# Router logits of a fused attention, mixture-of-experts and channel-mix kernel: stationary and moving operands swapped onto four column tiles, counts in three products, scatters through disjoint views

## The chip, the cores and the metric

The kernel runs on one core of one Trainium2 chip. A NeuronCore has five engines, each with its own queue of instructions: TensorE (PE; its weight loads are listed apart as PEld), VectorE (DVE), ScalarE (ACT), GpSimd (POOL) and SyncE (SP, which here only issues DMAs). The metric is the device time of one execution in microseconds, lower is better. Of several runs the median counts.

## The reference

Three stages follow one another, for a batch of 2 and a sequence of 768, all in fp32.

```python
# attention: 8 heads of 64, causal window of 96 keys plus 8 global keys, a bias by distance
scores = q @ k.T / 8 - slope[h] * dist ; masked ; a = softmax(scores) ; x = a @ v     # x: [2, 768, 512]
# mixture of experts: 8 experts, one of them for each token
logits = x @ w_gate                        # [.., 8]
local  = sigmoid(x @ w_local)              # [.., 1]
for each batch, for s in order:
    fresh = argmax(logits[s])
    e = fresh if s == 0 or local[s] < 0.5 else e_of_the_token_before
    out[s] = softmax(logits[s])[e] * (relu(x[s] @ w1[e]) @ w2[e])
# channel mix
xk, xr = mixes of x with the token before ; k = relu(xk @ w_k) ; y = sigmoid(xr @ w_r) * (k*k @ w_v)
```

A token may inherit the expert of the token before it, so routing needs a scan over the tokens in order. Since the softmax of the attention divides by a sum for each head, the kernel keeps x undivided and multiplies the logits of each head with that head's reciprocal.

## The kernel before, in words

The 1536 tokens are 12 tiles of 128. The attention part is a software pipeline over 24 iterations `i`, two for each tile (`t, g = divmod(i, 2)`, four heads each). In an iteration PE issues the transposes of the probabilities of the iteration before (`emit_pT`, lines 899 and 901, two PSUM banks of the name PT in turn), scores for later iterations (`emit_S`, line 866) or the transposes of the next k and q (line 823), and at every second iteration the products of probabilities and v (`emit_pv`, line 924), which run on two column tiles of 64. ACT does the exponentials (line 892), half of the evictions of transposed probabilities (`pt`, line 908; DVE does the other half, line 910) and the evictions of the transposed attention output `xT` (line 929). DVE adds the bias and takes the minimum (line 880). At odd iterations PE turns `xT` back (`turn_x`, line 182, into a bank PT) and DVE multiplies it into `X` (`route_x`, line 186), which empties that bank.

Routing runs beside this for groups of two tiles, six groups in all. Their steps are put at named points of later iterations (`at(i, point, ...)`; in an iteration the points come in the order Ra, Dm, Rb, Db, Rc, Dc), so the order on every engine is fixed by the program text. The steps that matter here:

- `route_lg` (line 200), at Rb of iteration `2 * g[-1] + 3`: for each of the two tiles four products with `xT` (128x128) as the stationary operand and a block-diagonal `wgb` of 18 columns (two heads, 8 experts and the local gate each) as the moving one. The result has tokens on partitions, and heads and experts along the free dimension.
- `route_max` (line 206 and after), at Dm of the next iteration: DVE scales by the reciprocals and adds over the heads.
- `route_rows`, `route_scan`, `route_turn`, `route_oh`: the scan over tokens on one partition, then a one-hot of the chosen expert (`OHr`).
- `route_sum` (lines 273 to 279): running counts of tokens for each expert, by products of one-hots with triangles of ones (`tri[:, 0]` lower triangle, `tri[:, 1]` all ones), with `acc` the sum of earlier groups. For two tiles these are five products of 8 columns (three in the first group, which has no `acc`), then the total counts.
- `route_pos`, then `scatter` (line 283): POOL writes the rows of X into `xs` in DRAM, sorted by expert. A scatter is issued where the queue `scq` holds one, at most one at each of two points of an iteration. After scatters 7 and 9 SP loads early rows of `xs` (line 948). The scatters all write the one tensor `xs`, so each waits for the one before it to land.

All the small PSUM results of routing share one bank of the name R. The sixth group is handled in the tail, where its logits are written with `route_lg` between products of the first expert. After that come the experts (products in three parts of fp32r, lines 641 to 643, with weights split by ACT at line 625 and by DVE), then the channel mix.

Of the kernel before, what the change touches and what calls it, by code (L numbers as in the profile page):

```python
# [7 lines left out]

F32 = mybir.dt.float32
# [3 lines left out]
ACTF = mybir.ActivationFunctionType  # L13
ALU = mybir.AluOpType
AX = mybir.AxisListType

P = 128
B, H, S, HD = 2, 8, 768, 64
D, E, F = 512, 8, 1024
NT = S // P  # L20
NTT = B * NT
KD = D // P
# [20 lines left out]
ROWS = sum(CAPS)  # L43
PRE = P
FREE = 4
NIN = 4
NI = 2 * NTT
NTAB = (5, 4)
# [5 lines left out]
class Net:  # L54
# [29 lines left out]
    def routing_consts(self):  # L84
        nc, c = self.nc, self.const
        self.wg = c.tile([P, KD, E + 1], F32, name="wg")
        nc.sync.dma_start(out=self.wg[:, :, 0:E], in_=self.i["w_gate"].rearrange("(k p) e -> p k e", p=P))
        nc.sync.dma_start(out=self.wg[:, :, E:E + 1], in_=self.i["w_local"].rearrange("(k p) e -> p k e", p=P))
        self.wgb = c.tile([P, KD, 2, E + 1], F32, name="wgb")
        nc.gpsimd.memset(self.wgb, 0.0)  # L90
        self.LS = c.tile([P, NTT, E + 1], F32, name="LS")
        self.RI = c.tile([P, NTT, H], F32, name="RI")
        self.MX = c.tile([P, NTT], F32, name="MX")
        self.OHr = c.tile([P, NTT, E], F32R, name="OH")
        self.OH = self.OHr.bitcast(F32)
        self.POS = c.tile([P, NTT], F32, name="POS")
        self.posi = c.tile([P, NTT], I32, name="posi")
        self.yposi = c.tile([P, NTT], I32, name="yposi")
        self.PE = c.tile([P, NTT], F32, name="PEX")
        self.caps = c.tile([8, E], F32, name="caps")  # L100
        self.bases = c.tile([8, E], F32, name="bases")
        nc.vector.memset(self.caps, 256.0)
        for r in (0, THIRD) + HALF:
            nc.vector.memset(self.caps[:, r:r + 1], float(CAPS[r]))
        nc.vector.tensor_scalar(self.bases, self.iota_e[0:8, :], 256.0, float(BASES[3] - 768), op0=ALU.mult, op1=ALU.add)
        nc.vector.memset(self.bases[:, 0:1], 0.0)
        for r in (1, 2) + tuple(range(HALF[0] + 1, E)):
            nc.vector.memset(self.bases[:, r:r + 1], float(BASES[r]))
        self.places = c.tile([8, E], F32, name="places")
        for p, k in enumerate(PLACES):  # L110
            nc.gpsimd.memset(self.places[:, p:p + 1], float(k))
        self.last = c.tile([8, E], F32, name="last")
        nc.vector.memset(self.last, float(P))
        nc.vector.memset(self.last[:, THIRD:THIRD + 1], float(LAST))
        self.second = c.tile([8, E], F32, name="second")
        nc.vector.memset(self.second, float(P))
        for r in HALF:
            nc.vector.memset(self.second[:, r:r + 1], float(LAST))
        self.elast = None
# [17 lines left out]
    def gate_rest(self):  # L137
        for a in range(2):
            r = slice(a * HD, (a + 1) * HD)
            self.nc.gpsimd.tensor_copy(self.wgb[r, :, a, :], self.wg[r, :, :])  # L140

    def mix_rest(self):
        for m in self.mu.values():
# [50 lines left out]
    def route_lg(self, g, t, xT, tag="R"):  # L194
        nc = self.nc
        if t == g[0]:
            self.lgp = self.bank(tag, 2 if tag == "PT" else 1)
        for kk in range(KD):
            o = ((t - g[0]) * H + 2 * kk) * (E + 1)
            nc.tensor.matmul(self.lgp[:, o:o + 2 * (E + 1)], lhsT=xT[:, kk, :],  # L200
                             rhs=self.wgb[:, kk, :, :].rearrange("p a c -> p (a c)"), start=True, stop=True)

    def route_max(self, pool, g):
        nc, n, t0 = self.nc, len(g), g[0]
        lh = pool.tile([P, n * H, E + 1], F32, tag="lh", bufs=1, name=f"lh{t0}")
        nc.vector.tensor_tensor(lh, self.lgp[:, 0:n * H * (E + 1)].rearrange("p (a c) -> p a c", c=E + 1),
                                self.RI[:, t0:t0 + n, :].rearrange("p a h -> p (a h)").unsqueeze(2).to_broadcast([P, n * H, E + 1]), op=ALU.mult)
        lp = self.LS[:, t0:t0 + n, :]
        nc.vector.tensor_reduce(lp, lh.rearrange("p (a h) c -> p a c h", h=H), axis=AX.X, op=ALU.add)
        mx = self.MX[:, t0:t0 + n]  # L210
        nc.vector.tensor_reduce(mx, lp[:, :, 0:E], axis=AX.X, op=ALU.max)
        ab = pool.tile([P, 2, n], F32, tag="ab", bufs=2, name=f"ab{t0}")
        fl = pool.tile([P, n], F32, tag="fl", bufs=2, name=f"fl{t0}")
        nc.vector.tensor_scalar(ab[:, 0, :].unsqueeze(2), lp[:, :, E:E + 1], ZCUT, None, op0=ALU.is_gt)
        eq = pool.tile([P, n, E], F32, tag="eq", bufs=2, name=f"eq{t0}")
        nc.vector.tensor_tensor(eq, lp[:, :, 0:E], mx.unsqueeze(2).to_broadcast([P, n, E]), op=ALU.is_ge)
        nc.vector.tensor_scalar(fl.unsqueeze(2), lp[:, :, E:E + 1], ZCUT, None, op0=ALU.is_le)
        if t0 % NT == 0:
            nc.vector.memset(ab[0:1, 0, 0:1], 0.0)
            nc.vector.memset(fl[0:1, 0:1], 1.0)  # L220
        self.mxs = (eq, ab, fl)
# [45 lines left out]
    def route_sum(self, pool, g):  # L267
        nc, n, t0 = self.nc, len(g), g[0]
        pp = self.bank("R", 1)
        for i in range(n):  # L270
            rest = [self.OHr[:, t0 + a, :] for a in range(i)] + ([self.acc] if self.acc is not None else [])
            o = pp[:, i * E:(i + 1) * E]
            nc.tensor.matmul(o, lhsT=self.tri[:, 0, :], rhs=self.OHr[:, t0 + i, :], start=True, stop=not rest)
            for a, x in enumerate(rest):
                nc.tensor.matmul(o, lhsT=self.tri[:, 1, :], rhs=x, start=False, stop=a == len(rest) - 1)
        one = self.tri[:, 1, 0:1].bitcast(F32)
        parts = [self.OHr[:, t, :].bitcast(F32) for t in g] + ([self.acc.bitcast(F32)] if self.acc is not None else [])
        for a, x in enumerate(parts):
            nc.tensor.matmul(pp[0:8, n * E:n * E + 1], lhsT=x, rhs=one, start=a == 0, stop=a == len(parts) - 1)
        self.pp = pp  # L280

    def scatter(self, X, t):
        self.nc.gpsimd.indirect_dma_start(self.xs, bass.IndirectOffsetOnAxis(ap=self.posi[:, t:t + 1], axis=0),  # L283
                                          X[t], None)

    def route_pos(self, pool, g):
# [291 lines left out]
def build(ctx, tc, ins, out):  # L578
# [2 lines left out]
    q, k, v = ins["q"], ins["k"], ins["v"]  # L581
    w1, w2 = ins["w1"], ins["w2"]
    n.xs = n.dram.tile([E * REG, D], F32, name="xs")
    ys = n.dram.tile([ROWS, D], F32, name="ys")
    rp = ctx.enter_context(tc.tile_pool(name="rp", bufs=1))
    wstack = ExitStack()
# [378 lines left out]
    def at(i, point, *fs):  # L965
        plan.setdefault((i, point), []).extend(fs)
# [2 lines left out]
        for f in plan.pop((i, point), ()):  # L969
            f()  # L970

    def lg(g):
        for t in g:
            n.route_lg(g, t, xTs[t])

    def pos(g):
        n.route_pos(ap2, g)
        scq.extend(g)
# [4 lines left out]
    for g in groups:  # L983
        i = 2 * g[-1] + 3
        lgg, mx, mx2, rows, scan, tn, oh, sm_, ps_, acc = (lambda f=f, g=g: f(ap2, g) for f in (
            lambda _, g: lg(g), n.route_max, n.route_max2, n.route_rows, n.route_scan, n.route_turn, n.route_oh, n.route_sum,
            lambda _, g: pos(g), n.route_acc))
        if g[-1] == NTT - 1:
            tail = mx, mx2, rows, scan, tn, oh, sm_, ps_
            continue  # L990
        at(i, "Rb", lgg)
        at(i + 1, "Dm", mx, mx2)
        if g[-1] == NTT - 3:
            tail8 = rows, scan, tn, oh, sm_, ps_, acc
            continue
        at(i + 1, "Rc", rows)
        if g[-1] == NTT - 5:
            at(i + 1, "Dc", scan)
            at(i + 2, "Ra", tn)
            at(i + 2, "Dm", oh)  # L1000
            at(i + 2, "Rb", sm_)
            at(i + 2, "Db", ps_, acc)
        else:
            at(i + 2, "Dm", scan)
            at(i + 2, "Rb", tn)
            at(i + 2, "Db", oh)
            at(i + 3, "Rb", sm_)
            at(i + 3, "Db", ps_, acc)
        if g[-1] in (5, 7):
            e = g[-1] == 7  # L1010
            at(i + 3, "Db", lambda e=e: n.order_a(ap2, "fg"[e], n.cnte if e else n.cnt6, n.fvec if e else None))
            at(*((i + 4, "Ra") if e else (i + 3, "Dc")), lambda e=e: n.order_b(ap2, "fg"[e], rp))
            at(i + 4, "Rb", lambda e=e: early_start(3 * e, e))

    with tc.manual_schedule():
# [96 lines left out]
        for i in range(NI - 1):  # L1112
# [46 lines left out]
                emit_pv(u, 1)  # L1159
            do(i, "Rc")  # L1160
            do(i, "Dc")
            if scq:
                scatter(scq.pop(0))
            if g == 1 and t + 2 < NTT:
                load("v", t + 2)
# [797 lines left out]
```

## Time and profile before

| what | value |
|---|---|
| median of 3 runs | 487.65 us (485.9, 487.65, 492.04) |
| the profiled execution's own time | 488.38 us |
| its span, first to last instruction | 486.3 us |
| mean granted TensorE clock | 0.99 |
| PE busy, share of the span | 469.6 us, 97% |
| PEld busy | 407.0 us, 84% |
| DVE busy | 344.4 us, 71% |
| ACT busy | 265.5 us, 55% |
| POOL busy | 114.4 us, 24% |

Matmuls are pipelined, and their ends are modelled, so what one costs in a row of them is read from the distance of the starts, not from its duration. In a timeline, `x4` means that a row holds four instructions that follow each other. `128*64 128x128` on PE means 128 rows and 64 columns of the array, with a moving operand of 128 partitions and 128 columns. A plain fp32 product shows as two instructions. The attention part ends near 118 us, the last group's routing near 134 us.

### The profile page before, as it was taken

Reading aid. Unit: us, or ns where it says so; the run is one execution under the profiler, and the core shown is the slowest. Engines: PE = TensorE matmul, PEld = TensorE weight load, DVE = VectorE, ACT = ScalarE, POOL = GpSimd, SP = SyncE. Lnnn points to the kernel's source line nnn. Section 1 sums busy time; section 2 is a strip of 40 time slices with the busy share of each in tenths; the row PEclk is TensorE's granted clock in tenths of the full one; section 3 lists DMA queues with packets and bytes.
Section 4 is the critical chain, followed back from the end, with each engine's and each line's share of the span. In section 5 each row is a group of like instructions: output and inputs, shape, how many; then the busy total and the mean of one; then the engine's idle time right before and its main releaser. Section 6 shows DMA issues by size and latency. Waiting matters only on the chain. (4 is left out here: it accounts for less than half of the span.)

```text
span 486.3 us, 9258 instructions
## 1 busy us (share of the span) xinstructions
PE 469.6 (97%) x3211; PEld 407.0 (84%) x3211; DVE 344.4 (71%) x911; ACT 265.5 (55%) x652; POOL 114.4 (24%) x200
## 2 busy tenths in 40 slices
PE   7999999889999999999999999999999999999994
PEld 5788888778788989878978887798989899898984
DVE  7877796696875885897898888797857768264301
ACT  4787876764536554757587776862433414152320
POOL 4111212112110000010010013051754918253220
PEclk9999998989999999999999999999999999999998
DMA  9998585962775978598699753003836442200001
GB/s 181 266 234 165 145 175 153 290 201 83 255 278 167 355 207 325 171 345 288 238 344 378 278 177 97 34 1 90 301 109 246 146 155 82 65 23 23 22 3 49
DMA packets 76492, 86.90 MB, mean 179 GB/s; under 512 B 50677, under 2 KB 50933, under 8 KB 76437
## 3 DMA queue, kind: packets, MB, share of 16 engines
q1 hardware_dynamic: 68176, 63.01, 42.3%
q0 software_dynamic: 4944, 17.17, 10.9%
q10 hardware_dynamic: 3316, 6.03, 3.4%
q8 instruction: 28, 0.46, 0.4%
q14 instruction: 28, 0.22, 0.2%
HBM read 73.49 MB, written 12.71 MB: 177 GB/s over the span
## 5 line engine op out<-in xcount | busy, mean ns | idle before, releaser
L625 ACT ACTIVATE whi<-wraw 128x512 fp32r<-128x512 f32 x128 | 72.5, 623 | 6.1 <-ACTq L717 2.3
L634 DVE TENSOR_TENSOR wlo<-wraw,whi 128x1024 fp32r<-128x1024 f32 x55 | 66.0, 1217 | 2.7 <-ACT whi L625 2.5
L1474 ACT ACTIVATE sq<-S 128x256 f32<-128x256 f32 x48 | 18.5, 385 | 74.4 <-PE S L643 71.3
L641 PE MATMUL S<-xkh,whi 128*128 128x256 f32 x192 | 54.5, 284 | 0.2 <-ACT whi L625 0.2
L643 PE MATMUL S<-xkh,wlo 128*128 128x256 f32 x192 | 53.6, 279 | 0.2 <-DVE wlo L630 0.2
L642 PE MATMUL S<-xkl,whi 128*128 128x256 f32 x192 | 53.5, 279 | 0.0
L1484 POOL TENSOR_TENSOR kl<-sq,kh 128x256 fp32r<-128x256 f32 x40 | 36.5, 921 | 71.1 <-issue 37.4
L1514 DVE TENSOR_TENSOR o<-O,sig 128x512 f32<-128x512 f32 (+1 forms) x13 | 8.4, 649 | 51.9 <-PE O L643 31.7
L642 PE MATMUL O<-wlo,kh 128*128 128x512 f32 (+1 forms) x104 | 39.3, 378 | 0.3 <-DVE wlo L630 0.3
L643 PE MATMUL O<-whi,kl 128*128 128x512 f32 (+1 forms) x104 | 39.3, 378 | 0.0
L641 PE MATMUL O<-whi,kh 128*128 128x512 f32 (+1 forms) x104 | 39.1, 376 | 0.0
L641 PEld LDWEIGHTS S<-xkh,whi 128*128 128x128 f32 x192 | 36.4, 190 | 0.7 <-ACT whi L625 0.4
L643 PEld LDWEIGHTS S<-xkh,wlo 128*128 128x128 f32 x192 | 36.0, 188 | 0.4 <-DVE wlo L630 0.4
L642 PEld LDWEIGHTS S<-xkl,whi 128*128 128x128 f32 x192 | 36.1, 188 | 0.3
L1475 DVE SCALAR_TENSOR_TENSOR sq<-S,sq 128x256 f32<-128x256 f32 x48 | 20.1, 420 | 16.4 <-ACT sq L1474 16.0
L1483 ACT ACTIVATE kh<-sq 128x256 fp32r<-128x256 f32 x48 | 19.7, 412 | 12.0 <-DVE sq L1475 12.0
L892 ACT ACTIVATE zbig<-zbig,nm 128x232 f32<-128x232 f32 (+1 forms) x48 | 22.4, 466 | 5.9 <-DVE nm L880 5.9
L283 POOL DMA_INDIRECT xs<-X,posi x12 | 12.5, 1045 | 53.1 <-DVE acc L301 21.1
L642 PEld LDWEIGHTS O<-wlo,kh 128*128 128x128 f32 x104 | 19.6, 188 | 4.6 <-DVE wlo L630 0.7
L641 PEld LDWEIGHTS O<-whi,kh 128*128 128x128 f32 x104 | 19.6, 188 | 3.8
L643 PEld LDWEIGHTS O<-whi,kl 128*128 128x128 f32 x104 | 19.6, 188 | 3.7
L892 ACT ACTIVATE peb<-peb,nm 128x232 f32<-128x232 f32 (+1 forms) x48 | 22.2, 463 | 0.0
(461 smaller groups left out, 1423.0 us busy)
## 6 DMA issues: line engine op xcount, KB each, us to landing
wraw<-in_moe_w_dram SPq DMA_DIRECT2D x64, 512.0 KB, 5.7
dwt<-in_moe_w_v_dram POOLq DMA_DIRECT2D x8, 512.0 KB, 4.6
z<-in_moe_w_k_dram SPq DMA_DIRECT2D x8, 512.0 KB, 4.2
z<-in_moe_w_v_dram SPq DMA_DIRECT2D x8, 512.0 KB, 4.8
ys<-yo ACTq DMA_DIRECT2D x13, 256.0 KB, 6.5
vn<-in_v_dram SPq DMA_DIRECT2D x12, 256.0 KB, 4.1
xn<-xs SPq DMA_DIRECT2D x12, 256.0 KB, 5.3
dwt<-in_moe_w_k_dram POOLq DMA_DIRECT2D x6, 512.0 KB, 6.8
```

Source lines behind the costliest of these rows:

```text
L283: self.nc.gpsimd.indirect_dma_start(self.xs, bass.IndirectOffsetOnAxis(ap=self.posi[:, t:t + 1], axis=0), X[t], None)
L625: nc.scalar.activation(out=whl[r, c][0][:, sl], in_=raws[r, c][:, sl], func=ACTF.Copy)
L634: nc.vector.tensor_tensor(lo, raws.pop((r, c)), hi.bitcast(F32), op=ALU.subtract)
L641: nc.tensor.matmul(out_, lhsT=ah, rhs=bh, start=first, stop=False)
L642: nc.tensor.matmul(out_, lhsT=ah, rhs=bl, start=False, stop=False)
L643: nc.tensor.matmul(out_, lhsT=al, rhs=bh, start=False, stop=last)
L892: nc.scalar.activation(out=pe, in_=pe, func=ACTF.Exp, scale=-1.0, bias=nm[:, h:h + 1], accum_out=sm[:, h:h + 1])
L1474: nc.scalar.activation(out=sq_, in_=ps[:, 0:TB], func=ACTF.Relu)
L1475: nc.vector.scalar_tensor_tensor(sq_, ps[:, 0:TB], 0.0, sq_, op0=ALU.max, op1=ALU.mult)
L1483: nc.scalar.activation(out=hh, in_=sq_, func=ACTF.Copy)
L1484: (nc.gpsimd if b else nc.vector).tensor_tensor(hl, sq_, hh.bitcast(F32), op=ALU.subtract)
L1514: nc.vector.tensor_tensor(o[:, a:z], ps[:, 0:z - a], sig[b, i][:, a:z], op=ALU.mult)
```

## The change

Three things change.

1. For groups 1 to 5 the logits are formed with `wgb` (now padded to 32 columns a block, `GW`) as the stationary operand and `xT` as the moving one. The four blocks `kk` go to the four column tiles of 32 (`tile_position`), so the result has heads and experts on partitions and tokens along the free dimension (`route_lgt`, at the old place Rb). ACT evicts it at Db (`route_lge`), and at Ra of the next iteration PE transposes it back (`route_lgb`), ahead of `route_max`. The sixth group keeps `route_lg`, with its blocks 32 columns apart.
2. `route_sum` forms the counts of both tiles in one product of 16 columns, adds `acc` in another and the first tile's one-hots to the second tile's counts in a third.
3. Each scatter writes through its own view of `xs` that is declared disjoint from the others, and at the end of an iteration up to two are issued instead of one.

```diff
-        self.wgb = c.tile([P, KD, 2, E + 1], F32, name="wgb")
+        self.wgb = c.tile([P, KD, GW], F32, name="wgb")
...
+    def route_lgt(self, pool, g, xTs):
+        nc, n = self.nc, len(g)
+        bank = self.bank("R", 1)
+        for i, t in enumerate(g):
+            for kk in range(KD):
+                nc.tensor.matmul(bank[kk * GW:(kk + 1) * GW, i * P:(i + 1) * P], lhsT=self.wgb[:, kk, :], rhs=xTs[t][:, kk, :],
+                                 start=True, stop=True, tile_position=(0, kk * GW))
+        self.lgp = bank
+
+    def route_lge(self, pool, g):
+        n = len(g)
+        self.lgt = pool.tile([P, 2, P], F32, tag="lgt", bufs=1, name=f"lgt{g[0]}")
+        self.nc.scalar.activation(out=self.lgt[:, 0:n, :], in_=self.lgp[:, 0:n * P].rearrange("p (a c) -> p a c", a=n), func=ACTF.Copy)
+
+    def route_lgb(self, pool, g):
+        self.lgp = self.bank("R", 1)
+        for i in range(len(g)):
+            self.nc.tensor.transpose(self.lgp[:, i * P:(i + 1) * P], self.lgt[:, i, :], self.ident)
...
     def route_sum(self, pool, g):
         nc, n, t0 = self.nc, len(g), g[0]
         pp = self.bank("R", 1)
-        for i in range(n):
-            rest = [self.OHr[:, t0 + a, :] for a in range(i)] + ([self.acc] if self.acc is not None else [])
-            o = pp[:, i * E:(i + 1) * E]
-            nc.tensor.matmul(o, lhsT=self.tri[:, 0, :], rhs=self.OHr[:, t0 + i, :], start=True, stop=not rest)
-            for a, x in enumerate(rest):
-                nc.tensor.matmul(o, lhsT=self.tri[:, 1, :], rhs=x, start=False, stop=a == len(rest) - 1)
+        parts = [(0, n, self.tri[:, 0, :], self.OHr[:, t0:t0 + n, :].rearrange("p a e -> p (a e)"))]
+        if self.acc is not None:
+            parts.append((0, n, self.tri[:, 1, :], self.acc.unsqueeze(1).to_broadcast([P, n, E])))
+        if n > 1:
+            parts.append((1, n, self.tri[:, 1, :], self.OHr[:, t0, :]))
+        for i, (a, z, w, x) in enumerate(parts):
+            nc.tensor.matmul(pp[:, a * E:z * E], lhsT=w, rhs=x, start=i == 0, stop=i == len(parts) - 1)
...
     def scatter(self, X, t):
-        self.nc.gpsimd.indirect_dma_start(self.xs, bass.IndirectOffsetOnAxis(ap=self.posi[:, t:t + 1], axis=0),
+        self.nc.gpsimd.indirect_dma_start(self.xviews[t], bass.IndirectOffsetOnAxis(ap=self.posi[:, t:t + 1], axis=0),
                                           X[t], None)
...
+    n.xviews = dram_disjoint_views(n.xs, NTT)
...
         at(i, "Rb", lgg)
+        at(i, "Db", lambda g=g: n.route_lge(ap2, g))
+        at(i + 1, "Ra", lambda g=g: n.route_lgb(ap2, g))
         at(i + 1, "Dm", mx, mx2)
...
-            if scq:
+            for _ in scq[:2]:
                 scatter(scq.pop(0))
```

The order of PE's instructions around the logits of group 2 before (a number behind a tile's name tells its buffers apart; `xT` is the undivided attention output, `R` the routing bank):

```order
L182 MATMUL PT_821<-ident,xT_802 128x128 x4
L200 MATMUL R_826<-wgb,xT_672 128x18 x4
L200 MATMUL R_826<-wgb,xT_802 128x18 x4
L899 MATMUL PT_846<-ident,zbig 128x128
L901 MATMUL PT_846<-ident,zbig 128x128
L899 MATMUL PT_846<-ident,peb_107 128x128
L901 MATMUL PT_846<-ident,peb_107 128x128
```

and after the change:

```order
L184 MATMUL PT_825<-ident,xT_807 128x128 x4
L210 MATMUL R_830<-xT_677,wgb 32x128 x4
L210 MATMUL R_830<-xT_807,wgb 32x128 x4
L923 MATMUL PT_852<-ident,zbig 128x128
L925 MATMUL PT_852<-ident,zbig 128x128
L923 MATMUL PT_852<-ident,peb_107 128x128
L925 MATMUL PT_852<-ident,peb_107 128x128
L923 MATMUL PT_857<-ident,zbig 128x128
L925 MATMUL PT_857<-ident,zbig 128x128
L923 MATMUL PT_857<-ident,peb_108 128x128
L925 MATMUL PT_857<-ident,peb_108 128x128
L222 MATMUL R_862<-ident,lgt_847 128x128 x2
```

The products stand where they stood. Two transposes of `lgt` come behind the eight transposes of probabilities.

The order of ACT's instructions at the same place, before (lines 892 and 916 are the exponentials, 908 and 932 the eviction of transposed probabilities):

```order
L892 ACTIVATE zbig,sm_703<-zbig,nm_702 128x232
L892 ACTIVATE peb_108,sm_703<-peb_108,nm_702 128x232
L892 ACTIVATE zbig,sm_836<-zbig,nm_835 128x232
L892 ACTIVATE peb_105,sm_836<-peb_105,nm_835 128x232
L908 ACTIVATE pt_1_860<-PT_851 128x512
```

and after:

```order
L916 ACTIVATE zbig,sm_708<-zbig,nm_707 128x232
L916 ACTIVATE peb_108,sm_708<-peb_108,nm_707 128x232
L217 ACTIVATE lgt_847<-R_830 128x256
L916 ACTIVATE zbig,sm_840<-zbig,nm_839 128x232
L916 ACTIVATE peb_105,sm_840<-peb_105,nm_839 128x232
L932 ACTIVATE pt_1_869<-PT_857 128x512
```

The eviction of the logits stands ahead of the two exponentials of the next iteration, and these ahead of the eviction of the probabilities.

SP's issues around the first early load of `xs` (`xe`), before (`wraw` are expert weights, `vn` and `vp` tiles of v):

```order
L594 ISA
L594 DMA wraw_3_1517<-in_moe_w_dram 128x1024
L806 DMA vn_1570<-in_v_dram 128x8x64
L596 ISA
L596 DMA wraw_4_1593<-in_moe_w_dram 128x2x512
L948 ISA
L948 DMA xe_1599<-xs 128x512
```

and after:

```order
L618 ISA
L618 DMA wraw_3_1532<-in_moe_w_dram 128x1024
L972 ISA
L972 DMA xe_1584<-xs 128x512
L830 DMA vn_1586<-in_v_dram 128x8x64
L620 ISA
L620 DMA wraw_4_1609<-in_moe_w_dram 128x2x512
```

The early load of `xs`, which waits for scatter 7, now stands ahead of a tile of v and of the first piece of w2 (128x2x512).

## Rows read from the trace of the kernel before

**Rows 1.** Stretches: us; PE, PEld, DVE, ACT, POOL busy (count); granted clock; DMA share, GB/s.
```profile
40.00:50.00 10.00, 10.00 (x120) 9.19 (x118) 7.45 (x32) 7.36 (x24) 2.44 (x3) 1.00 0.68 153
90.00:100.00 10.00, 7.82 (x87) 6.94 (x89) 8.48 (x37) 8.10 (x24) 1.73 (x3) 1.00 0.74 220
```

**Rows 2.** Timeline of PE, group 2: start us, us, line, op, tiles, shape, count.
```profile
44.81 1.86 PE L200 MATMUL R<-wgb,xT 128*128 128x18 f32 x16
46.52 0.31 PE L899 MATMUL PT<-ident,zbig 128*128 128x128 f32 x1
46.66 0.27 PE L901 MATMUL PT<-ident,zbig 128*128 128x128 f32 x1
46.77 0.27 PE L899 MATMUL PT<-ident,peb 128*128 128x128 f32 x1
```

**Rows 3.** Timeline of PE: into the products of probabilities and v, and out.
```profile
30.66 0.60 PE L823 MATMUL S<-ident,qn 128*128 128x128 f32 x4
31.19 0.44 PE L924 MATMUL O<-pt,vn 128*64 128x128 f32 x4
31.46 0.39 PE L924 MATMUL O<-pt,vp 128*64 128x128 f32 x4
31.68 0.39 PE L924 MATMUL O<-pt,vn 128*64 128x128 f32 x4
...
96.11 0.39 PE L924 MATMUL O<-pt,vp 128*64 128x128 f32 x4
96.43 0.33 PE L899 MATMUL PT<-ident,zbig 128*128 128x128 f32 x1
96.60 0.27 PE L901 MATMUL PT<-ident,zbig 128*128 128x128 f32 x1
```

**Rows 4.** Timeline of ACT, groups 2 and 3; idle before and releaser in brackets.
```profile
47.68 0.60 ACT L908 ACTIVATE pt<-PT 128x512 f32<-128x512 f32 x1 [2.37 <-PE PT L901]
...
63.54 0.39 ACT L908 ACTIVATE pt<-PT 128x256 f32<-128x256 f32 x1 [1.95 <-PE PT L899]
```

**Rows 5.** The page, groups of instructions: busy us, mean ns, idle before, releaser.
```profile
L892 ACT ACTIVATE zbig<-zbig,nm 128x232 f32<-128x232 f32 (+1 forms) x48 | 22.4, 466 | 5.9 <-DVE nm L880 5.9
```

**Rows 6.** Timeline of PE, group 4.
```profile
78.79 1.96 PE L200 MATMUL R<-wgb,xT 128*128 128x18 f32 x16 [0.24 <-DVE fi L339]
...
81.30 0.42 PE L899 MATMUL PT<-ident,zbig 128*128 128x128 f32 x1
...
83.99 0.54 PE L924 MATMUL O<-pt,vn 128*64 128x128 f32 x4
```

**Rows 7.** Timeline of DVE, group 4.
```profile
79.94 0.67 DVE L186 TENSOR_TENSOR X<-PT,RI 128x512 f32<-128x512 f32 x1
```

**Rows 8.** Timeline of PE, group 5.
```profile
103.93 0.30 PE L899 MATMUL PT<-ident,zbig 128*128 128x128 f32 x1 [0.15 <-DVE X L186]
```

**Rows 9.** Timeline of PE: counts of group 3, and the wait after group 4.
```profile
72.08 0.25 PE L273 MATMUL R<-OH,tri 128*128 128x8 f32 x1
...
72.53 0.25 PE L275 MATMUL R<-acc,tri 128*128 128x8 f32 x1
...
93.10 0.30 PE L899 MATMUL PT<-ident,zbig 128*128 128x128 f32 x1 [1.28 <-DVE mm L291]
```

**Rows 10.** Stretches behind the logits of groups 4 and 5, columns as in rows 1.
```profile
80.50:84.50 4.00, 4.00 (x27) 3.67 (x28) 2.86 (x18) 2.05 (x7) 0.00 (x0) 0.57 0.97 270
104.50:108.50 4.00, 4.00 (x38) 3.67 (x38) 3.83 (x19) 3.04 (x8) 0.00 (x0) 0.57 0.96 293
```

**Rows 11.** Scatters, line 283: who waited for it, us, times.
```profile
  POOL xs L283: 14.1, 5
```

**Rows 12.** Timeline of SP: its DMA issues.
```profile
90.68 2.10 SPq L596 DMA_DIRECT2D wraw<-in_moe_w_dram  x1
102.28 0.36 SPq L948 DMA_DIRECT2D xe<-xs  x1
```

**Rows 13.** Timeline of ACT in the tail.
```profile
123.19 1.14 ACT L625 ACTIVATE whi<-wraw 128x512 fp32r<-128x512 f32 x2
```

More of the change, by code (lines that the diff above doesn't have):

```diff
@@ L5 @@
 from concourse import mybir
+from concourse.ap import dram_disjoint_views
 from concourse._compat import with_exitstack
@@ L45 @@
 FREE = 4
+GW = 32
 NIN = 4
@@ L139, in gate_rest @@
             r = slice(a * HD, (a + 1) * HD)
-            self.nc.gpsimd.tensor_copy(self.wgb[r, :, a, :], self.wg[r, :, :])
+            self.nc.gpsimd.tensor_copy(self.wgb[r, :, a * (E + 1):(a + 1) * (E + 1)], self.wg[r, :, :])
     def mix_rest(self):
@@ L198, in route_lg @@
         for kk in range(KD):
-            o = ((t - g[0]) * H + 2 * kk) * (E + 1)
+            o = ((t - g[0]) * KD + kk) * GW
             nc.tensor.matmul(self.lgp[:, o:o + 2 * (E + 1)], lhsT=xT[:, kk, :],
-                             rhs=self.wgb[:, kk, :, :].rearrange("p a c -> p (a c)"), start=True, stop=True)
+                             rhs=self.wgb[:, kk, 0:2 * (E + 1)], start=True, stop=True)
+    def route_lgt(self, pool, g, xTs):
[14 more added lines that the diff above has]
+            self.nc.tensor.transpose(self.lgp[:, i * P:(i + 1) * P], self.lgt[:, i, :], self.ident)
     def route_max(self, pool, g):
@@ L205, in route_max @@
         lh = pool.tile([P, n * H, E + 1], F32, tag="lh", bufs=1, name=f"lh{t0}")
-        nc.vector.tensor_tensor(lh, self.lgp[:, 0:n * H * (E + 1)].rearrange("p (a c) -> p a c", c=E + 1),
-                                self.RI[:, t0:t0 + n, :].rearrange("p a h -> p (a h)").unsqueeze(2).to_broadcast([P, n * H, E + 1]), op=ALU.mult)
+        nc.vector.tensor_tensor(lh.rearrange("p (m a) c -> p m a c", a=2),
+                                self.lgp[:, 0:n * P].rearrange("p (m r) -> p m r", r=GW)[:, :, 0:2 * (E + 1)].rearrange("p m (a c) -> p m a c", a=2),
+                                self.RI[:, t0:t0 + n, :].rearrange("p t (k a) -> p (t k) a", a=2).unsqueeze(3).to_broadcast([P, n * KD, 2, E + 1]), op=ALU.mult)
         lp = self.LS[:, t0:t0 + n, :]
@@ L970, in do @@
             f()
-    def lg(g):
-        for t in g:
-            n.route_lg(g, t, xTs[t])
     def pos(g):
@@ L985, in build @@
         lgg, mx, mx2, rows, scan, tn, oh, sm_, ps_, acc = (lambda f=f, g=g: f(ap2, g) for f in (
-            lambda _, g: lg(g), n.route_max, n.route_max2, n.route_rows, n.route_scan, n.route_turn, n.route_oh, n.route_sum,
+            lambda _, g: n.route_lgt(ap2, g, xTs), n.route_max, n.route_max2, n.route_rows, n.route_scan, n.route_turn, n.route_oh, n.route_sum,
             lambda _, g: pos(g), n.route_acc))
```

## The prediction

> **What bounds the kernel now.** The page's busy times have PE as the busiest engine by far, so I went on to the stretches of 10 us: in 40 to 50 us PE has no idle time at all at full clock, in 90 to 100 us it is busy for 7.82 of 10 us [rows 1]. So up to about 70 us whatever PE no longer has to issue shortens the time, and later in the attention part something else sometimes holds it. Then I went to the stretch of one routing group in PE's timeline, to the same engine where it already works in column tiles, to what ACT and DVE do there, and to the granted clock.
>
> Where PE issues the logits of a group, 16 instructions start between 44.81 and 46.52 us: 1.71 us, 0.107 us each, though each moves only 18 columns [rows 2]. (A plain fp32 product is two instructions, a transpose one, which is how 8 products of the source become 16.) That is the step of a 128x128 transpose, 0.11 us [rows 2], which loads as many stationary columns. So these products cost what their loading costs, and swapping the operands, so that wgb with 32 columns stands and x with 128 columns moves, attacks the right thing.
>
> **The change, part by part.** Times are against the profiled execution, 488.38 us with a span of 486.3; the median of the three timed runs is 487.65, 0.15% less, and they spread from 485.9 to 492.04, so I don't correct for it. 2% of it, 9.8 us, is about what a measurement of this kernel can tell from no change.
>
> *Logits of groups 1 to 5* (the sixth keeps its old form). Removed: 1.71 us of PE a group. Added: 16 instructions on four column tiles, then two transposes. The nearest row is the product of probabilities and v, which runs on two column tiles of 64: four instructions of 128 columns take 0.22 us (31.46 to 31.68), so 0.11 us for each and two at a time [rows 3]. If as many go at once as there are tiles, 16 take 4 x 0.11 = 0.44 us; if two go at once, 0.88; if none overlap, 1.76. I take 0.44, because the two tiles of the row overlap without a loss, and keep the other ends for the rivals.
>
> Here the Trainium skill weighs a little against me: TensorE: Matmul & The Clock Gate, section Measured speedup vs the span model, has 2.38 times for three column tiles instead of 3. Scaled to four tiles that estimate is 1.71 / 3.17 = 0.54 us a group, which would put my time 0.4 us higher; the row of this trace, which shows no loss with two tiles, decides.
>
> Entering column tiles costs something. The last 128x128 transpose before 31.19 starts at 30.66 + 3 x 0.11 = 30.99; the step to 31.19 is 0.20 instead of 0.11, and the first four take 0.27 instead of 0.22. Leaving: from 96.11 + 0.11 to 96.43 it is 0.21, and then 0.17, instead of 0.11 [rows 3]. That is 0.14 in and 0.16 out, 0.30 a group (none if the tiles join without a gap, twice this if four tiles drain longer than two). The two transposes of lgt are 0.22. New cost 0.44 + 0.30 + 0.22 = 0.96, saving 0.75 a group where PE is the bound.
>
> *What ACT now does.* It gets an eviction of 128x256 in each group, 0.39 us by the nearest one [rows 4], queued ahead of the first two exponentials of the next iteration and waiting for the logits. At these places, as groups 2 and 3 show, ACT waits 2.37 and 1.95 us for PE before its next PT eviction [rows 4]. In group 2 the logits would be out at 44.81 + 0.14 + 0.44 + 0.27 = 45.66; eviction and the two exponentials behind it (0.47 each [rows 5]) end near 47.1, and the PT eviction starts then instead of at 47.68. So ACT comes out ahead. On PE the transposes of lgt stand behind eight transposes of probabilities (0.88 us), which covers 0.27 + 0.39 us; in group 3, at the start of the second batch, there are only four (0.44; its tiles take half the columns), and PE may wait 0.2 us. Groups 1 to 3 give 0.75 + 0.75 + 0.5 = 2.0 us.
>
> *Groups 4 and 5.* There the second set of probability transposes needs the PT bank that DVE empties into X. In group 4 X ends at 79.94 + 0.67 = 80.61 and the transposes start at 81.30 [rows 6, 7]; with the logits done 0.9 us sooner they still wait for X, and then come the 0.22 us of lgt's: 0.1 gained at full clock. In group 5 PE already waits for X at 103.93 [rows 8]: the logits save nothing, and lgt adds 0.22 on PE beside a DVE that is behind anyway. I book 0.1 for both together.
>
> *Counts.* Five products become three, each 128 stationary columns: 72.08 to 72.53 is four steps, 0.11 each [rows 9]. Two go in each group, one in the first, which has no acc: 0.11 + 5 x 0.22 = 1.2 us of PE. In group 4 PE then runs into a wait of 1.28 us for DVE [rows 9], which takes its 0.2 back. Gain 1.0.
>
> *Scatters.* Five of twelve waited on the landing of the one before, 14.1 us in total, and the only engine on the list of those that waited for a scatter is POOL itself [rows 11]. Nothing on PE, ACT or DVE waits for them, so I cost this part at nothing. Moving scatters 6 and 7 together pulls the first early load of xs on SP ahead of a load of v and of w2's first piece. That piece was issued at 90.68, and the load of xs at 102.28 [rows 12]; ACT first splits it at 123.19 [rows 13]. Even if it had to wait until 102.28, 20 us would be left. If this cover were gone, each us that w2 came late would be a us of PE.
>
> *The clock.* In 80.5 to 84.5 and in 104.5 to 108.5 us the granted clock averages 0.57, that is mostly the 1.2 GHz level [rows 10]; PE is busy throughout, so each of these costs 0.43 x 4 = 1.7 us of PE's work. What PE did before each: turned x, issued the 16 thin logit products, and transposed. Groups 1 to 3 did the same without a fall, so it is not certain in either kernel. With the thin products gone PE spends 0.44 us on products of 128 columns in their place. I take it that the first fall goes. It delayed the transposes that start at 81.30, and the next product started at 83.99 [rows 6]; at full clock 81.30 would have been near 81.1 and 83.99 near 82.5, so it is worth 1.5. The second falls where DVE is late and I book nothing for it. Bounds: 0 (both stay) and 3.4 (both go and both paid in full).
>
> Sum: 2.0 + 0.1 + 1.0 + 0 + 1.5 = 4.6 us. 488.38 - 4.6 = **483.8 us**, 0.8% under the median.
>
> **Rivals.**
> 1. *Two tiles at a time, not four.* 0.88 + 0.30 + 0.22 = 1.40 us a group saves 0.31 in groups 1 and 2, 0.1 in group 3 and nothing later: 0.7 + 1.0 + 1.5 = 3.2, so 485.2 us. For it: the row shows just two at a time, because there are just two tiles. Against: nothing in it shows a limit. 20%.
> 2. *The clock falls as before*, because most of what PE does there, the transposes, stays. 2.0 + 0.1 + 1.0 = 3.1, so 485.3 us. For it: transposes make up most of what stands before both falls. 25%.
> 3. *Slower: the column tiles don't overlap.* If loading or moving on one tile holds the next, 16 instructions take 1.76 us, and with 0.30 and 0.22 a group takes 2.28, 0.57 more than now. All five places pay it (in group 4 the logits would then end after X): 2.9 - 1.0 = 1.9 us, with the clock as it was 490.2 us. It decides once a group's 16 take over 1.71 - 0.30 - 0.22 + 1.0/5 = 1.39 us. Against: the pairs that overlap in [rows 3]. 8%.
> 4. *ACT becomes late.* If the exponentials queued behind lgt's eviction reach PE late, the saving turns into a wait at the next iteration's transposes: 0.4 us (the eviction) in five places, 2.0 of the 4.6 us, so 485.8 us. Against: ACT's waits of about 2 us in [rows 4]. 10%.
> 5. *It does more than I book*: both clock falls go and both pay, and the gap at a change of tiles is half as long: 1.9 + 0.5 on top, 481.4 us. 10%.
>
> My forecast itself gets 27%. The range of 480.5 to 488.0 takes in the forecast and rivals 1, 2, 4 and 5 with the spread of single runs; rival 3 and outliers are left out. Over 2% faster (under 477.9) would need more than all the PE time that the thin products and both clock falls leave to win at once: 4%. Over 2% slower (over 497.4) needs five times rival 3: 3%. Within 2%: 93%.
>
> **What would show it.** The 16 instructions of a group, from the first to the start of the next transpose: about 0.7 us if four go at once, 1.1 for two, 2 for none. Between the last probability transpose and lgt's first no idle time on PE in groups 1 and 2, a short one in group 3. ACT's PT eviction earlier against the logits than now. The scatters 1 us apart on POOL with no change on PE. Full clock behind group 4's logits. Three steps of 0.11 us in the counts. I would be wrong if PE's idle time in 20 to 70 us rose by as much as its instructions shrank, or if the expert part, whose PE time the change doesn't touch, became shorter or longer.

## The result and the profile after

Six runs of the changed kernel have a median of 482.83 us (482.3 to 485.56), six of the kernel before on the same chip 488.12 us. The ratio is 0.9893, 95% interval 0.9854 to 0.9933: 3.3 to 7.1 us less. The forecast was 483.8, within 2%. The sum came out, but partly by luck: the counts and the clock did not bring in the runs what was booked for them, and the experts' products, which the sum left out, made up for it, as the account below shows.

The profiled execution is the slowest of the six, 485.56 us with a span of 483.7. Most of what sets it above the median lies at the start. PE's timeline of it, and then of the same kernel profiled a second time (482.82 us, span 480.8; called "again" from here):

```profile
13.11 0.42 PE L923 MATMUL PT<-ident,zbig 128*128 128x128 f32 x1
13.32 0.42 PE L923 MATMUL PT<-ident,peb 128*128 128x128 f32 x1
```
```profile
10.20 0.27 PE L923 MATMUL PT<-ident,zbig 128*128 128x128 f32 x1
10.31 0.27 PE L923 MATMUL PT<-ident,peb 128*128 128x128 f32 x1
```

The same two transposes start 0.21 us apart in the one and 0.11 in the other. Until 14.1 us PE runs at half its rate, as at 1.2 GHz, though the granted clock reads 1.00 there; it costs nearly 3 us. Three of the fourteen profiles show such a late start, so I compare with "again".

Group 2 of the profiled execution, which answers to [rows 2]:

```profile
45.61 0.66 PE L184 MATMUL PT<-ident,xT 128*128 128x128 f32 x4
46.20 0.65 PE L210 MATMUL R<-xT,wgb 128*32 128x128 f32 x16
46.77 0.33 PE L923 MATMUL PT<-ident,zbig 128*128 128x128 f32 x1
...
48.02 0.30 PE L923 MATMUL PT<-ident,zbig 128*128 128x128 f32 x1 [0.59 <-DVE X L188]
...
48.48 0.38 PE L222 MATMUL R<-ident,lgt 128*128 128x128 f32 x2
```

The 16 instructions take 0.57 us from the first start to the next transpose, instead of 1.71. Then something new: the second set of probability transposes waits 0.59 us for X. DVE in the same place, and PE's longest waits on its list (us, times, longest):

```profile
47.18 0.69 DVE L188 TENSOR_TENSOR X<-PT,RI 128x512 f32<-128x512 f32 x1 [0.55 <-DMA xs<-X,posi]
```
```profile
PE PT L923 <- DVE X L188: 3.5, 5, 1.4
PE O L1051 <- DVE warm L73: 1.5, 1, 1.5
PE PT L923 <- DVE mm L314: 1.5, 1, 1.5
```

In the kernel before, transposes waited for X 0.6 us in all, 0.45 of it ahead of group 1, where the changed kernel waits as long; new are the waits in groups 2 and 3 and the longer ones in groups 4 and 5. PE's timeline of before, then of "again" at the same place and in group 3:

```profile
20.74 0.30 PE L899 MATMUL PT<-ident,zbig 128*128 128x128 f32 x1 [0.45 <-DVE X L186]
```
```profile
20.58 0.30 PE L923 MATMUL PT<-ident,zbig 128*128 128x128 f32 x1 [0.45 <-DVE X L188]
...
61.10 0.30 PE L923 MATMUL PT<-ident,zbig 128*128 128x128 f32 x1 [0.38 <-DVE X L188]
```

The X of group 2 also waits for a transfer: it is the fourth, there are three buffers, and scatter 0 has to land first.

Places that answer to [rows 6, 8, 9], PE's timeline of "again":

```profile
78.64 0.30 PE L923 MATMUL PT<-ident,zbig 128*128 128x128 f32 x1 [0.74 <-DVE X L188]
...
80.29 0.33 PE L948 MATMUL O<-pt,vn 128*64 128x128 f32 x2
...
89.31 0.30 PE L923 MATMUL PT<-ident,zbig 128*128 128x128 f32 x1 [1.51 <-DVE mm L314]
...
100.13 0.30 PE L923 MATMUL PT<-ident,zbig 128*128 128x128 f32 x1 [1.36 <-DVE X L188]
```

Between [rows 6]' 81.30 and 83.99 lay a clock fall; from 78.64 to 80.29 there is none, 1.65 us instead of 2.69, with the 0.22 us of lgt's transposes now among them. Behind the counts of group 4 PE now waits 1.51 us, where it waited 1.28. Where the same instruction of PE starts, us, and how much earlier than before:

| instruction | before | whole change, again | logits alone |
|---|---|---|---|
| scores, first after the start | 25.35 | 24.93 (-0.42) | 25.33 (-0.02) |
| k turned, behind group 1's logits | 30.23 | 29.01 (-1.21) | 29.41 (-0.82) |
| the same, group 2 | 47.42 | 46.09 (-1.33) | 45.95 (-1.48) |
| the same, group 3 | 63.34 | 61.57 (-1.77) | 61.21 (-2.13) |
| second set, group 4 | 81.30 | 78.64 (-2.65) | 78.28 (-3.01) |
| product with v, group 4 | 83.99 | 80.29 (-3.70) | 79.94 (-4.05) |
| behind the counts of group 4 | 93.10 | 89.31 (-3.80) | 88.95 (-4.15) |
| second set, group 5 | 103.93 | 100.13 (-3.80) | 99.78 (-4.15) |
| first transpose after the second fall | 107.92 | 102.81 (-5.11) | 102.45 (-5.47) |
| experts, early | 168.67 | 164.19 (-4.48) | 163.67 (-5.00) |
| experts | 304.17 | 300.24 (-3.93) | 298.92 (-5.25) |
| experts, late | 434.27 | 428.61 (-5.65) | 427.34 (-6.93) |

### The profile page after: what moved, and what is told of

It reads as the page before. It is cut to its first block, busy times and chain, and to the rows that moved or that the text cites. A ratio compares the mean times of both kernels' runs of the same rounds, so it can differ in the third digit from the quotient of the medians.

```text
span 483.7 us, 9264 instructions
## 1 busy us (share of the span) xinstructions
PE 464.4 (96%) x3210; PEld 400.1 (83%) x3210; DVE 345.5 (71%) x911; ACT 267.2 (55%) x657; POOL 115.5 (24%) x200
```

## The experiments

**Each part alone.** The edits are the hunks of the diff above: `route_sum` alone; `xviews` with `scq[:2]` alone; `wgb`, `route_lgt`, `route_lge`, `route_lgb` and `route_max` alone; and everything but the scatters.

> The kernel before with the counts alone in three products (thin logits, scatters one at a time as before). My terms: five products less in four of five groups of 0.11 us each, one in the first, together 1.0 us: 487.1 us, ratio 0.998; the mean granted clock as before, near 0.990, because the thin logit products stay. Rival: DVE, on which the transposes after group 4 and 5 wait anyway, takes it back, 488.1, ratio 1.000.

Measured: 486.56 us median, ratio 0.997 (0.9943 to 0.9997). In the profile the counts pay nothing. It is 0.30 us ahead at the place of 81.30 us of before and 0.07 at 93.10: what the products save, 0.2 to 0.3 us at a time, comes back at a later wait for DVE. By 107.92 it has gained another 1.5 us, because a second clock fall did not come. That explains this profile and not the medians, since the mean granted clock of the runs is the same (0.9950, and 0.9951 for the kernel before); where their 1.95 us come from stays open.

> The kernel before with the scatters alone changed (twelve views of xs, two at a time). My term: 0, so 488.1 us, ratio 1.000; POOL no longer waits 14.1 us for landings, and no other engine gains. Rival: the landings did hold something that the list of waits does not show, the early loads of xs for instance, and at least 1.5 us of the 5.3 measured for the whole change come from here, 486.6. Second rival: X on DVE now waits for a landing and this part costs 0.5 us.

Measured: 487.61 us, ratio 0.9985 (0.9965 to 1.0004). As I booked it: nothing clear of the noise.

> The kernel before with the logits alone on column tiles (five counts products, scatters one at a time on one view). My terms: 2.1 us of PE time and 1.5 us for a clock fall that goes, 484.5 us, ratio 0.9926, with a mean granted clock of 0.994 to 0.997 in its runs as the whole change shows. Rival clock: the falls have nothing to do with the thin products; the mean clock stays near 0.990 and the time is 486.0. Rival X: the second set of probability transposes waits 3.5 us for X in five groups, so that PE gains under 1 us and the time is 487.2 without the clock.

Measured: 481.37 us, ratio 0.9883 (0.9842 to 0.9923). By the medians the logits alone give at least what the whole change gives. The table above shows where: from group 2 on this kernel is ahead of "again" by 0.15 to 0.5 us, though it started 0.4 us behind, and neither has a clock fall in its attention part. Another 0.8 us comes at 304.17, where "again" waits 1.16 us for a tile of the experts on DVE (yg) and this kernel 0.15. The rival "X" is right for groups 4 and 5 alone. From the list of PE's waits:

```profile
PE PT L920 <- DVE X L187: 2.6, 3, 1.4
```

The three are 0.45 us at the place ahead of group 1 that waits in the kernel before too, 0.74 in group 4 and 1.37 in group 5. In groups 1 to 3 there is none, and they gain 0.80, 0.66 and 0.65 us.

> The whole change without its scatters (logits on column tiles, counts in three products, scatters one at a time on one view). My terms: the same as the whole change, ratio 0.989 to 0.9905, 483.2 us. Rival: the scatters carry 1 us or more, so that this one stands at 0.9915 or above. Second rival: without the pairs X has no landing to wait for and this is 0.5 us faster than the whole change, 0.988.

Measured: 482.74 us, ratio 0.99 (0.9861 to 0.9939). The same as the whole change within the noise, so the scatters carry nothing here that shows. The second rival falls: X still waits 0.65 us for a landing, with scatters one at a time. Of the eight profiles with three products in the counts of group 1 it waits in seven, of the six with five in one, for 0.3 us. The counts of group 1 let the next loads of v and k go out sooner, while DVE decides when scatter 0 starts (41.20 us before, 41.17 with the counts alone); that they crowd the scatter is argued, not shown.

**X first.** 

```
             emit_min(i + 1)
-            if g == 1 and i > 1:
-                n.route_x(ap, X, t - 1)
```
The two removed lines go ahead of `emit_min(i + 1)`.

> The whole change, with DVE computing X ahead of the four minima of the next iteration instead of behind them, in every iteration that has an X. In the profile of the whole change the second set of probability transposes waits for X: 0.74 us in group 4, 1.50 at its counts, 1.36 in group 5, and smaller ones in groups 1 to 3. The four minima take 1.28 us, so X comes 1.28 us sooner. My theory: these waits are where part of the saving went, and PE gets 2 to 2.5 us of them back: 480.3 us, ratio 0.984; the list of PE's waits shows under 1 us on X. Rival: the minima, 0.6 us later, make the exponentials and the next probability transposes late by as much, and the time stays at 482.8. Third: shorter pauses of PE also take away the clock fall that is left, another 1.5 us, 479.

Measured: 487.1 us, ratio 0.9995 (0.997 to 1.0021). All of the gain was lost, and neither theory nor rivals saw how. The profiled execution is the slowest of the twelve, with a late start and a clock fall at 52.1 us. DVE and then PE in group 2:

```profile
49.84 0.69 DVE L188 TENSOR_TENSOR X<-PT,RI 128x512 f32<-128x512 f32 x1 [4.19 <-DMA xs<-X,posi]
```
```profile
50.68 0.30 PE L923 MATMUL PT<-ident,zbig 128*128 128x128 f32 x1 [2.00 <-DVE X L188]
```

X comes 1.28 us sooner on DVE's queue and stands there 4.19 us for scatter 0 to land, now with the four minima behind it. PE loses 2.0 us by it. Later the order pays: PE's waits at the places of 78.64, 89.31 and 100.13 us of "again" shrink from 0.74, 1.51 and 1.36 us to none, 0.20 and none. A new wait of 1.0 us for the ranking (dgf on DVE) takes a part back; from 63.34 to 103.93 us of before this kernel gains 1.3 us on "again".

**The order of the column tiles.**

```
-        for i, t in enumerate(g):
-            for kk in range(KD):
+        for kk in range(KD):
+            for i, t in enumerate(g):
```

> The whole change with the 16 instructions of a group in another order: the four of a column tile one behind the other, then the next tile, instead of going round the four tiles. The same work and bytes. My theory: a tile starts when the instructions ahead of it have been issued, so tiles overlap only where one gives way to the next: 13 steps of 0.11 us, 1.4 us from the first start to the last, instead of 0.35; 0.9 to 1.0 us longer in groups 1 to 3 and 0.2 to 0.7 in 4 and 5 where PE waits for X anyway: 485.8 us, ratio 0.9955. Rival: the order does not matter, because an engine with four tiles starts whatever is next on a free tile; 0.44 us as now, 482.8 us.

Measured: 483.03 us, ratio 0.9911 (0.9882 to 0.9939). My theory fell. PE's timeline:

```profile
43.55 0.66 PE L210 MATMUL R<-xT,wgb 128*32 128x128 f32 x16
44.15 0.33 PE L923 MATMUL PT<-ident,zbig 128*128 128x128 f32 x1
```

It takes 0.60 us instead of 0.57. The trace gives no tile to an instruction, but the four starts that come together every 0.11 us are 13 ns apart here instead of 7, as if PE still had four tiles at work, though the four of one tile stand one behind the other in the program. That they overtake is inferred from the starts, not seen.

**Which counts bring the pause.** The edit is `if t0 == 6:` ahead of the old five products, else the new three.

> The whole change, with the counts of group 4 (tiles 6 and 7) alone in five products as before. In the profile of the whole change PE's pause behind these counts is 1.50 us and the granted clock falls to 0.50 for 3.4 us right behind it; with the logits alone changed the pause is 1.28 us and no fall follows. Theory pause: the two products that were saved there only lengthened a pause of PE, and the clock fell behind it; with them back the fall goes, 481.0 us, ratio 0.985. Rival chance: where the clock falls depends on more than this pause (with the scatters left out it fell behind group 5 instead), and a fall comes in most runs anyway: 482.7 us, ratio 0.989.

Measured: 482.37 us, ratio 0.9894 (0.9866 to 0.9921). The pause is 1.28 us again (89.79 us, on DVE's `mm`), and PE loses nothing by it: the two products fit into the wait. But "again", with a pause of 1.51 us, had no fall in its profile either, so such a pause alone does not make one.

> The whole change once more, as the measure for the other three on the same chip: 482.8 us, ratio 0.989, one clock fall of 3.4 us in most runs; the run that gets TensorE to its full clock late (at 14 us instead of 6) is 3 us longer.

Measured: 483.86 us, ratio 0.9939 (0.9914 to 0.9964); seven of its twelve runs lie between 482.5 and 483.9, five between 485.5 and 486.8, as a late start of 3 us would make them. This interval and that of the first runs just overlap.

**X first, from group 4 on.** The same edit with `i >= 17` for the new place and `1 < i < 17` for the old, on the logits alone and on the whole change.

> The logits alone on column tiles (counts and scatters as before), with X ahead of the four minima on DVE from group 4 on, where three X are in flight no longer: not in groups 1 to 3, where X earlier than now has to wait for a scatter to land. My theory: as in the kernel with X first everywhere, the three late pauses shrink by 0.9, 1.3 and 1.3 us and 1.4 us come back as waits for the ranking and for pt: 2.1 us under the logits alone, 479.3 us, ratio 0.983. Rival: the later minima cost as much as X gains, 481.4, 0.988.

Measured: 482.0 us (lowest 480.06), ratio 0.9858 (0.9836 to 0.9881).

> The whole change with X ahead of the minima from group 4 on only. My theory: 2.1 us under the whole change, and the 0.22 us that the counts save in group 4 is then no longer swallowed by a wait for X: 480.5 us, ratio 0.9855; still above the logits alone with the same order, because in groups 1 to 3 X gives the counts' saving back. Rival: the counts now pay their 1.0 us and this one is the fastest, 478.5, ratio 0.981.

Measured: 481.72 us (lowest 480.17), ratio 0.9897 (0.9861 to 0.9933), with two of six runs at 485.01 and 486.65, as after a late start; the profiled run, 480.17 us, is 2.65 us under "again".

The theories said 479.3 and 480.5. By the place of 103.93 us of before the profiles are 3.2 and 3.6 us ahead of those without the edit, but 0.65 and 0.75 of that stood at 63.34, before the edit acts: it gives 2.5 and 2.8. The first kernel then loses 3.0 us again, in a wait for the early load of xs and in a clock fall right behind. From the list of its PE's waits, and its SP:

```profile
PE S L672 <- DMA xe<-xs: 2.6, 1, 2.6
```
```profile
100.53 0.36 SPq L969 DMA_DIRECT2D xe<-xs  x1
```

In the whole change with the same edit the load goes out 7.4 us sooner, and PE does not wait for it; one scatter at a time makes it late (101.87 us against 96.91 in the whole change without and with the pairs, both profiles with a late start):

```profile
93.17 0.34 SPq L972 DMA_DIRECT2D xe<-xs  x1
```

So in these two profiles two scatters at a time keep 2.6 us, which they did not before PE was faster. The runs do not show it: the medians are 482.0 and 481.72 us, the lowest 480.06 and 480.17.

**lgt between the sets.** On the logits alone with X first from group 4 on:

```
                 emit_pT(i - 1, 0)
+                do(i, "Ra0")
                 emit_pT(i - 1, 1)
-        at(i + 1, "Ra", lambda g=g: n.route_lgb(ap2, g))
+        at(i + 1, "Ra0", lambda g=g: n.route_lgb(ap2, g))
```

> The logits alone on column tiles with X first from group 4 on, and the two transposes of lgt issued between the two sets of probability transposes instead of behind both. In the profile of the whole change lgt is out 0.1 us before the first set ends in group 2 and 0.1 us after it in group 3, and PE then waits 0.59 and 0.39 us for X: the 0.22 us of these transposes would lie in that wait. My theory: 0.2 us in groups 1 to 3 each, 0.5 us under the same kernel without this, 478.8 us, ratio 0.982. Rival: PE waits for lgt where it waited for X, 479.3, 0.983.

Measured: 481.86 us, ratio 0.9858 (0.9838 to 0.9879): no difference from the same kernel without it. The theory fell: in group 2 the transposes of lgt start 1.15 us behind the first logit (44.51 to 45.66 us) and the second set right after them, with no wait for X. Where the counts are as before, there is no wait in groups 1 to 3 to lie in. The rival is right in kind: PE's weight loads now wait for lgt in all five groups, 0.37 us in group 3 and 1.0 in all. On the whole change, where there is a wait for X, it was not tried.

**One product more in the kernel before.** `warm(1, 8)` behind the third `warm`.

> The kernel before with one more product of 8 columns among the first ones, at a place where PE is idle for 0.5 us anyway. It asks why the experts' products, which no kernel here changes, step at 118 ns in 40 to 43 of 100 cases in the three kernels with thin logits and in 9 to 24 of 100 in the others (113 ns for the rest): about 1.6 us of the time. Theory place: the step depends on where the products stand in the program, and any shift can change it; here the share falls to 25 or lower and the time by up to 1.6 us, ratio 0.997 to 0.998. Rival: the share stays at 40 or more and the time at 1.000, and something else about the kernels with thin logits sets it.

Measured: 487.82 us, ratio 1.0007 (0.9984 to 1.003). The share of slow steps is 46 of 100, so a shift by one product does not change it. This profile had another surprise, the stretches of [rows 10] in a program with the thin products at the same places:

```profile
80.50:84.50 4.00, 4.00 (x52) 3.70 (x51) 3.13 (x18) 2.50 (x7) 0.05 (x1) 1.00 0.98 271
104.50:108.50 4.00, 2.67 (x28) 2.13 (x25) 3.93 (x15) 2.50 (x8) 0.00 (x0) 1.00 0.82 229
```

No fall at all. PE is then early enough to wait 1.3 us for the early load of xs, which gives half of it back.

## Why the prediction came out

**Logits, groups 1 to 3, booked 2.0: right.** 0.80 + 0.66 + 0.65 = 2.1 us with the logits alone. Four tiles go at once: 0.57 us from the first start to the next transpose; with 0.09 by which the step ahead and 0.06 by which the step behind are longer than 0.11, 0.73 against 0.74 booked for products and both changes of tile. The ratio that the Trainium skill has (TensorE: Matmul & The Clock Gate, Measured speedup vs the span model) put the products alone at an estimated 0.54; in the trace they take 0.46, the 0.57 less what the step out is longer than 0.11, which decides for four without a loss. Rivals 1 and 3 are out; so is rival 4: on PE's list no wait up to 120 us is for an exponential. Its weight loads waited for lgt once, 0.6 us in group 3, and there X, which PE also needed, came 0.16 us after lgt ("again").

**Groups 4 and 5, booked 0.1: right in kind.** Group 5 gave nothing (-4.15 before and after it). Group 4 gave 0.4: 0.88 by 81.30, less an estimated 0.25 for the half microsecond of the fall that lay ahead of 81.30 and less lgt's 0.22 behind it.

**What is late next: missed.** I named the wait for X in groups 4 and 5 alone. In the whole change it came in groups 2 and 3 as well, 0.59 and 0.39 us, with 0.55 us on DVE for a landing in group 2, a wait that I had costed at nothing because only POOL was on the list of before. It came with the counts: the logits alone have no such wait.

**Counts, booked 1.0: wrong, in the profiles they pay nothing.** The products shrank as said, three steps of 0.11 (group 4's start at 89.14, 89.25 and 89.36 in the profiled execution). But the savings came back at the next waits for DVE, and in group 2 0.5 us more went for the landing: against the logits alone "again" goes from 0.40 us ahead at the start to 0.35 behind by the place of 93.10. I had let only group 4 take its share back. It is not that the logits had used up the slack between PE and DVE, for with the thin products the counts pay no more (0.07 us by 93.10). That the whole change is slower than the logits alone (482.83 and 483.86 against 481.37) fits, but the intervals of the ratios overlap.

**Scatters, booked 0: right**, alone and in the whole. The cover I named, 20 us at w2, was not the thin one. That is the early load of xs: with the logits alone it goes out at 98.28 us, 5.5 us before PE uses it. Its landing is not in the trace; where PE did wait for this load, it went on 3.0, 4.6 and 5.6 us after the issue (X first late on the logits alone, lgt between the sets, and the padded kernel before).

**The clock, booked 1.5: right against the one profile, not borne out by the runs.** From [rows 6] to "again" the stretch with the first fall shrinks by 1.05 us although lgt's 0.22 has come into it; with the 0.25 ahead of 81.30 that makes my 1.5. The second, of which I had booked nothing, gives 1.3, of which 0.3 goes back by 117 us. But with its two falls the profile that I started from was an unusual execution: it has a mean granted clock of 0.990, and of 63 later runs of the same kernel only 10 have 0.990 or less. Over these 63 the mean is 0.9956, over 19 runs of the whole change 0.9958, each with a standard error under 0.0005. So the change saves 0.1 us of lost clock in an average run, 0.7 at most, and not 1.5: rival 2 had the condition right, and its 485.3 left out the experts' 1.7 below. (All of these have in them a fall in the last microseconds, which every profile shows.)

The profiles alone mislead here. At 80 to 85 us a fall shows in three of four with thin logits and in none of ten with column tiles, but the padded kernel before had none, and four of the ten have one elsewhere. The profiled execution is one of them, behind PE's wait of 1.50 us at 91.93:

```profile
80.50:84.50 4.00, 3.26 (x44) 3.10 (x45) 3.67 (x20) 3.33 (x11) 0.00 (x0) 1.00 0.97 307
92.50:96.50 4.00, 4.00 (x37) 3.67 (x37) 3.40 (x14) 3.84 (x11) 1.97 (x2) 0.57 0.37 135
```

The others lie at 52.1 us (behind a wait of 2.00), at 102.8 (behind 1.37 for X) and at 103.8 (behind the 2.6 us for xs); "again" has waits of 1.51 and 1.36 and no fall. All three profiles with a late start have one, of the seven others one, which may be chance. What a fall costs where it lies is read from before and the padded kernel, which issue the same instructions there: 2.69 and 1.40 us from 81.30 to the product with v, 3.99 and 2.46 from 103.93 to 107.92, so 1.3 and 1.5 us. What decides in one run stays open.

**The experts, said to stay as they are: wrong.** From 304.17 to 434.27 us of before "again" gains 1.7 us in products that nothing changed; see below.

**The sum.** The logits' 2.1 and 0.4 and the experts' 1.7 make 4.2 us, and the two sets of runs of the whole change measured 5.3 and 3.6. Of the 4.6 booked, the counts' 1.0 and the clock's 1.5 are not in it. That a term which I had ruled out took their place is luck.

## What to carry to other kernels

Before two savings on one engine are added up, find the wait that each runs into next. Here DVE took back all that the counts saved; a product saved ahead of a wait is worth nothing. A transfer that no one waits for has only as much cover as the engines ahead leave it, so cost it again at the faster time; pairing the scatters was worth 0 at the kernel before, and up to 2.6 in a profile where PE came 7 us sooner. And a profile is one execution: before a term is booked on an event in it, such as a clock fall, see from the mean granted clock of other runs how often it comes. The whole change with X first from group 4 on (481.72 us, lowest 480.17) has the lowest profile, 478.3 us of span; the one that the ratios set apart from the whole change as it ran later is the logits alone with X first, 0.9858 (0.9836 to 0.9881) against 0.9939 (0.9914 to 0.9964), though it overlaps with that of the first runs.

## What the runs showed of the hardware

Four column tiles of 32 work at once: 16 instructions take 0.57 us, and 0.60 in another order of the program.

TensorE has two paces at full granted clock. The experts' products of 256 columns, in the same place of the program, PE's timeline of before and of "again":

```profile
401.60 0.36 PE L641 MATMUL S<-xkh,whi 128*128 128x256 f32 x1
401.80 0.28 PE L642 MATMUL S<-xkl,whi 128*128 128x256 f32 x1
401.91 0.28 PE L643 MATMUL S<-xkh,wlo 128*128 128x256 f32 x1
402.03 0.28 PE L641 MATMUL S<-xkh,whi 128*128 128x256 f32 x1
402.15 0.28 PE L642 MATMUL S<-xkl,whi 128*128 128x256 f32 x1
402.27 0.28 PE L643 MATMUL S<-xkh,wlo 128*128 128x256 f32 x1
402.38 0.28 PE L641 MATMUL S<-xkh,whi 128*128 128x256 f32 x1
```
```profile
396.58 0.37 PE L665 MATMUL S<-xkh,whi 128*128 128x256 f32 x1
396.79 0.28 PE L666 MATMUL S<-xkl,whi 128*128 128x256 f32 x1
396.91 0.28 PE L667 MATMUL S<-xkh,wlo 128*128 128x256 f32 x1
397.02 0.28 PE L665 MATMUL S<-xkh,whi 128*128 128x256 f32 x1
397.13 0.28 PE L666 MATMUL S<-xkl,whi 128*128 128x256 f32 x1
397.25 0.28 PE L667 MATMUL S<-xkh,wlo 128*128 128x256 f32 x1
397.36 0.28 PE L665 MATMUL S<-xkh,whi 128*128 128x256 f32 x1
```

From the second row to the last it is 0.588 us and 0.571 unrounded: five steps of 118 ns, and one of 118 with four of 113. Whole rows of 46 products keep one pace or the other after the transposes that precede them. In the four profiles with thin logits 40 to 46 of 100 steps are slow, in the ten with column tiles 9 to 24. Between 304.17 and 434.27 us of before this makes 0.9 us on the products of 256 columns, and 1.1 on those of 512, 232.5 ns apart before and 228.9 in "again": it covers the 1.7 us. Since moving the program by one product changed nothing, I suspect where the tiles lie in memory, which lgt and the wider wgb shift; this was not tried.
